# Moving key loads, two weight tiles' conversions and three operand loads in a fused attention and MLP kernel

## The chip, the cores and the metric

The kernel runs on one core of a Trainium2 chip, as one launch. The metric is device time in microseconds (us). A core has five engines that run their own instruction streams: TensorE (PE in the profile; its weight loads are PEld), VectorE (DVE), ScalarE (ACT), GpSimd (POOL) and SyncE (SP), which here only issues DMA transfers. The streams wait for each other through semaphores.

## The reference

Attention over four batches and eight heads (576 positions, 64 wide) with a decay from cumulated logarithms and a causal mask; its result, 2304 x 512, goes through two feed-forward layers. The weights of both layers arrive as float64, and the kernel converts them itself from their words.

```
scores = scale * q @ k.T                      # per head, 576 x 576
decay  = cum[:, None] - cum[None, :]          # cum = cumsum(log(clip(f, 1e-4, 1)))
attn   = softmax(where(causal, -1e9, scores + decay)) @ v
x      = attn, heads side by side             # 2304 x 512
h      = maximum(x @ w_in, 0)                 # 2304 x 2048
x      = (h * h) @ w_out                      # 2304 x 512
y      = (sigmoid(x @ w_gate) * (x @ w_val)) @ w_out2
```

## The kernel before

Each matmul operand is held as a high and a low part (fp32r), and a product takes three matmuls: high by high, high by low, low by high. Large products are made with seven block products in place of eight. The instruction order on each engine is the order in which the program calls the instructions (a manual schedule), and nearly every load and store goes through SyncE's one queue, in order. A DMA transfer also takes one of eight completion lanes in turn (DMAHW0 to 7).

**Attention** handles 16 pairs of heads p. A list, `ORDER`, gives the steps of one iteration with a lag in pairs, so three pairs are in work at a time. `load(p, which)` (L319) issues the loads of a pair: q and v in three pieces each (L335 twice, L339), k from the fourth pair on in four pieces for a transpose on DVE (L329). q and k have two buffers each, so pair p + 2 reuses the buffer of pair p. `cr_load` (L343) brings the decay rows of a pair into `cr`; in the setup these rows come from DVE's scan, in `pts`. `TQ` (L488) transposes q on TensorE and then loads q of pair p + 2; `TKv` transposes k on DVE; `kl` (L537) subtracts k's high part on POOL and then loads k of pair p + 2.

**The up stage** (first layer, x by w_in, relu and square) has eight blocks u of ten groups. A group is 12 matmuls (L240), then relu and square on ACT (L252, L253), block sums on DVE (L213), and stores of the `gt` tiles to DRAM by `g_spill` (L226; tiles of ten buffers). Beside it runs a list of weight pieces, `units`: a piece is loaded (L118 or L123) into one of two raw buffers, converted by ACT (L132) and four DVE operations (L150 to L160), and then, by its kind, made into high and low parts `hl` of w_in (ACT L179, POOL L183), kept as w_out, or stored to DRAM again as a gate or value tile (L862). A block has four pieces, two of w_in for the next block and two of w_out, or five, with a gate or value tile at the end.

**The down stage** (by w_out) has 84 steps of 12 matmuls (L1145): seven products k, three column ranges jj, four depth pieces w. Step i takes a tile `gl` loaded from DRAM (`d_load`, L819, three buffers) and split into high and low parts `gg` (`d_split`: ACT L825, then DVE L826, three buffers). Loop i splits for step i + 2. The first three loads and splits stand in the last block of the up stage. After step 3 the sums of the first product are copied by ACT and DVE out of PSUM into `pa0`, a tile in memory that the up stage used. The order of the loads in this loop:

```
        if i == NW - 1:
            g_spill(len(spill))
...
        while loaded[1] <= i + (4 if 57 <= i < 78 else 3):
...
            d_load(loaded[1])
            loaded[1] += 1
        if i == 2:
            g_spill(len(spill) // 2)
        if i > 0:
            d_split(i + 2)
```

The stages behind these, the gated layer and the output product, are not touched.

Of the kernel before, what the change touches and what calls it, by code (L numbers as in the profile page):

```python
# [41 lines left out]
def kernel(  # L42
# [17 lines left out]
    NP = BH // 2  # L60
# [250 lines left out]
    TP = 3  # L311
# [59 lines left out]
    def setup():  # L371
        nc.vector.memset(qk[1]["kh"].bitcast(F32)[:, 0:256], 0.0)
        nc.vector.memset(one_l.bitcast(F32), 0.0)
        for r in range(2):
            nc.vector.memset(one_l.bitcast(F32)[64 * r:64 * r + 64, 128 * r:128 * r + 128], 1.0)
        nc.vector.memset(cum_s.bitcast(F32)[:, 2 * S:3 * S], 0.0)
        for t in sm_t:
            nc.vector.memset(t[:, 9:13], 1.0e-9)
        nc.vector.memset(nm_t[0][:, 9:11], 0.0)
        for r in range(2):  # L380
            nc.vector.memset(nm_t[0][64 * r:64 * r + 64, 9 + r:10 + r], 1.0)
        busy(16)
        nc.sync.dma_start(out=f_sb, in_=f.rearrange("b h s -> (b h) s"))
        make_identity(nc, ident)
        for nm_ in "qk":
            for t in nat[nm_]:
                nc.gpsimd.memset(t[64:128, NF, :, :], 0.0)
        nc.scalar.activation(out=sm_t[0][0:1, 0:1], in_=one_l.bitcast(F32)[0:1, 0:1], func=AF.Ln)
        load(0, "qk", nc.scalar)
        nc.vector.tensor_scalar(f_sb, f_sb, 1.0e-4, 1.0, op0=ALU.max, op1=ALU.min)  # L390
        nc.vector.tensor_reduce(out=nm_t[0][:, 0:1], in_=ident[:, 0:111:22], axis=mybir.AxisListType.X, op=ALU.add)
        nc.vector.tensor_scalar(one_l, one_l.bitcast(F32), nm_t[0][:, 0:1], None, op0=ALU.mult)
        nc.scalar.activation(out=f_sb, in_=f_sb, func=AF.Ln)
        nc.scalar.activation(out=sm_t[0][0:BH, 0:1], in_=f_sb[:, 0:1], func=AF.Exp)
        nc.vector.tensor_tensor_scan(out=cum_f, data0=f_sb, data1=f_sb, initial=0.0, op0=ALU.add, op1=ALU.min)
        nc.vector.tensor_copy(cum_s[:, 0:S], cum_f)
        nc.vector.tensor_tensor(
            out=cum_s[:, S:2 * S], in0=cum_f, in1=cum_s.bitcast(F32)[:, 0:S], op=ALU.subtract
        )
        for d in qk:  # L400
            nc.gpsimd.memset(d["cr"].bitcast(F32), 0.0)
        for t in nat["v"]:
            nc.gpsimd.memset(t[64:128, NF, :, :], 0.0)
        for t in pt_t:
            nc.gpsimd.memset(t[:, 2 * POFF[NF] + S:2 * POFF[NF] + PC], 0.0)
        cum_v = cum_s.bitcast(F32).rearrange("p (t s) -> p t s", t=3)
        load(1, "q")
        cr_load(0, cum_v)
        load(1, "k")
        cr_load(1, cum_v)  # L410
        nc.gpsimd.memset(maskc, 0.0)
        nc.gpsimd.affine_select(
            out=maskc[:, MD:MD + 128], in_=maskc[:, MD:MD + 128], pattern=[[-1, 128]],
            compare_op=ALU.is_ge, fill=BIG, base=0, channel_multiplier=1,
        )
        for r in range(2):
            nc.gpsimd.affine_select(
                out=maskc[64 * r:64 * r + 64, S - REM:S], in_=maskc[64 * r:64 * r + 64, S - REM:S],
                pattern=[[-1, REM]], compare_op=ALU.is_ge, fill=BIG, base=0, channel_multiplier=1,
            )  # L420
# [67 lines left out]
    def TQ(p):  # L488
        x = ps2()
        if p < TP:  # L490
            live["kt", p] = ps2()
        if p > 2:
            live["s4", p - 1] = ps2()
            s4_decay(p - 1)
        live["q", p] = transpose_in(nat["q"][p % 2], x)
        if p + 2 < NP and p != 1:
            load(p + 2, "q")

    def qh(p):
# [37 lines left out]
    def kl(p, late):  # L537
        if late == (p < TP):
            d, eng = qk[p % 2], nc.vector if late else nc.gpsimd
            eng.tensor_tensor(out=d["kl"], in0=live.pop(("k", p)), in1=d["kh"].bitcast(F32), op=ALU.subtract)  # L540
            if not late and p + 2 < NP:
                load(p + 2, "k")

    def S01(p):
        s = live.pop(("s01", p))
# [197 lines left out]
    for it in range(min(lags), NP + max(lags)):  # L743
# [6 lines left out]
        for nm_, lag in steps:  # L750
            p = it - lag
# [79 lines left out]
    for u in range(NU):  # L831
        us = [("in", 2 * u + 2), ("in", 2 * u + 3)] if u < NU - 1 else []
        us += [("out", 2 * u), ("out", 2 * u + 1)]
        if 1 <= u <= 4:
            us.append((("gate", 0), ("gate", 1), ("val", 0), ("val", 1))[u - 1])
        at0 = (0, 3, 5, 7, 9) if len(us) == 5 else (0, 3, 6, 9)
        for x, o in zip(us, at0):
            for ph in range(3):
                when.setdefault(2 * GU * u + 2 * GU * (o + ph) // 12, []).append((len(units), ph))
            units.append(x)  # L840
    NX = len(units)
    loaded = [0, 6]
# [241 lines left out]
    for i, (k_, jj, w) in enumerate(steps):  # L1084
        if i == NW - 1:
            g_spill(len(spill))
            u1.close()
            gts.close()
            wi0.close()
            at_p = dn.enter_context(tc.tile_pool(name="at", bufs=2, side="right", reuse_waits="tile"))  # L1090
            wtmp_p[0] = w2s.enter_context(tc.tile_pool(name="tmp2", bufs=4, reuse_waits="tile"))
            raws = [raw_p.tile([128, 1024], F32, tag="raw", name=f"raw{n}") for n in range(2)]
            wt_p = w2s.enter_context(tc.tile_pool(name="wt", bufs=1, reuse_waits="tile"))
            wring = []
            pus = ExitStack()
            pu_p = pus.enter_context(tc.tile_pool(name="pu", bufs=1, reuse_waits="tile"))
            pu = {}
            for n in (1, 2, 3, 0):
                t = pu_p.tile([128, 4, BT], F32, tag=f"pa{n}", name=f"pa{n}")
                pu[n, 0], pu[n, 1] = t[:, 0:2, :], t[:, 2:4, :]  # L1100
            for n in range(3):
                pu[n, 2] = pu_p.tile([128, 2, BT], F32, tag=f"pb{n}", name=f"pb{n}")
            dd.update({n: t_src(3, n) for n in range(2)})
            dd[2], gl_more = (t[:, 0:2 * BT].rearrange("p (c t) -> p c t", c=2) for t in raws)
        if i == 57:
            gl_free.insert(0, gl_more)
        while loaded[1] <= i + (4 if 57 <= i < 78 else 3):
            if loaded[1] > 81:
                gl_free[:] = [t for t in gl_free if t is not gl_more]
# [3 lines that stand above are left out]
            g_spill(len(spill) // 2)  # L1113
        if i > 0:
            d_split(i + 2)
        if i == 8:
            wf_sums(NW - 1, nc.vector)
        if i in SUBS:
            n, wc = SUBS[i]
            a11, a2 = part(wc, 0, 0), part(wc, 1, n)  # L1120
            nc.vector.tensor_tensor(out=a11 if n else a2, in0=a2, in1=a11, op=ALU.subtract)
        if k_ < 6:
            if jj == 1 and w == NW - 1:
                prep_sums(k_ + 1, 0)
            if jj == 2:
                if w < NW - 1:
                    prep_sums(k_ + 1, w + 1)
                prep(k_ + 1, w)
        if late:
            late.pop(0)()  # L1130
        if i == K6:
            fa, fb = (
                wf_p.tile([128, 1024 * n], F32R, tag=f"wf{x}", name=f"f{x}") for x, n in enumerate((5, 3))
            )
            tt[0, 2], tt[0, 3], tt[0, 4] = quad(fa[:, 0:1536]), quad(fa[:, 1536:3072]), quad(fb[:, 0:1536])
            wring.append([t.rearrange("p (h n) -> p h n", h=2) for t in (fb[:, 1536:3072], fa[:, 3072:5120])])
        for fn in D1X.get(i, ()):
            fn()
        ws, s = aop[k_, w], gg.pop(i)
        for u in range(2):  # L1140
            for c in range(2):
                o = bank((BASE[k_] + 2 * jj + c) % 8)[:, 0:BT]
                cs = slice(c * 128, (c + 1) * 128)
                for x, (a, b_) in enumerate(((0, 0), (0, 1), (1, 0))):
                    nc.tensor.matmul(  # L1145
                        o, lhsT=ws[:, a, u, cs], rhs=s[:, b_, u, :],
                        start=(k_ in (0, 2, 5) and w == u == x == 0), stop=(w == NW - 1 and u == 1 and x == 2),
                        skip_group_check=k_ in (1, 3, 4, 6),
                    )
                if w == NW - 1 and u == 1:  # L1150
                    d_post(k_, jj, c, o)
# [183 lines left out]
    for n, (z, key, m) in enumerate(items):  # L1335
# [12 lines left out]
        elif m % 2:  # L1348
            at(*slot(z + 6), *[part_fn(w_sum, key, m // 2, x) for x in range(4)])
            for x in range(4):  # L1350
                p = 42 * (m // 2) + x - 1
# [353 lines left out]
```

## Time and profile before

| what | value |
|---|---|
| time, median of 3 runs | 946.87 us (946.37 to 947.45) |
| the profiled execution's own time | 948.93 us |
| its span, first to last instruction | 947.1 us |
| TensorE busy | 938.8 us, 99% of the span |
| VectorE busy | 731.7 us, 77% |
| ScalarE busy | 553.6 us, 58% |
| GpSimd busy | 308.8 us, 33% |
| TensorE clock granted | 1.00 of full speed over the run |

The profile is of one execution. Attention lasts until about 175 us, the up stage until 367, the down stage until 543, the gated layer and the output product to the end. Shares of busy time are averages over these stages; the time follows the engine that the others wait for in each, and that is TensorE almost everywhere.

### The profile page before, as it was taken

To read this page: it belongs to the slowest core of one execution; us is meant where nothing else is said; L and a number is where in the kernel's file an instruction comes from. 1 tells how busy PE (TensorE), PEld (TensorE's weight loads), DVE (VectorE), ACT (ScalarE), POOL (GpSimd) and SP (SyncE) were. 2 spreads that over 40 slices of the span, in tenths; PEclk is the share of its full clock that TensorE was granted. 3 is DMA by queue.
4 is the path that set the end of the run, shared out by engine and by line. 5 is a ranking of instruction groups with operands and counts; after the bars stand their busy time and mean duration, and the time that the engine had idled before them with its cause. 6 is when DMAs were issued, how large, how long until landed. Compare 5 with 4: busy or idle time off the path is not lost.

```text
span 947.1 us, 17435 instructions
## 1 busy us (share of the span) xinstructions
PE 938.8 (99%) x6058; PEld 872.4 (92%) x6058; DVE 731.7 (77%) x1485; ACT 553.6 (58%) x1113; POOL 308.8 (33%) x384
## 2 busy tenths in 40 slices
PE   8999999999999999999999999999999999999998
PEld 7888888888888889999999999999999999889998
DVE  8999998267666766787888988767666677698895
ACT  7889998366655665556566565544445455353432
POOL 7898998012121110010002446524344342200000
PEclk9999999999999999999999999999999999999999
DMA  5654440388888989767776512433333346864441
GB/s 126 145 120 93 91 80 14 101 263 261 281 261 282 288 287 315 209 196 210 227 236 194 149 64 95 139 115 126 121 113 126 136 151 212 258 217 140 150 133 69
DMA packets 185167, 160.83 MB, mean 170 GB/s; under 512 B 81112, under 2 KB 158252, under 8 KB 185080
## 3 DMA queue, kind: packets, MB, share of 16 engines
q1 hardware_dynamic: 184648, 159.54, 56.0%
q8 instruction: 47, 0.77, 0.3%
q14 instruction: 40, 0.33, 0.1%
q10 hardware_dynamic: 432, 0.20, 0.1%
HBM read 102.93 MB, written 56.73 MB: 169 GB/s over the span
## 4 chain that ended last, share of the span: by engine, by line
PE 77%; DMA 8%; DVE 6%; ACT 3%; issue 3%; POOL 2%; SPq 1%; DVEq 0%; ACTq 0%; POOLq 0%
PE ps L1199 27%; PE ps L1145 17%; PE ps L1545 9%; PE ps L240 5%; PE pa L646 4%; PE pa L475 4%; PE ps L1421 3%; PE pa L612 3%; DMA gl<-g 2%; DMA g<-gt 2%; DMA wraw<-in_moe_w_in_dram 2%; DVE gt L213 1%; DVE wtmp L155 1%; PE pa L240 1%; ACT gt L253 1%
## 5 line engine op out<-in xcount | busy, mean ns | idle before, releaser
L240 PE MATMUL ps<-xT,hl 128*128 128x512 f32 (+1 forms) x912 | 186.8, 367 | 0.3 <-POOL hl L183 0.3
L240 PEld LDWEIGHTS ps<-xT,hl 128*128 128x128 f32 x912 | 158.2, 189 | 28.9 <-POOL hl L183 0.7
L1145 PE MATMUL ps<-gg,ao 128*128 128x384 f32 x1008 | 175.6, 334 | 0.6 <-DVE gg L826 0.6
L1145 PEld LDWEIGHTS ps<-gg,ao 128*128 128x128 f32 x1008 | 174.6, 188 | 1.4 <-DVE gg L826 1.0
L601 POOL TENSOR_TENSOR pt<-pt,sm 128x128 f32<-128x128 f32 (+2 forms) x142 | 104.5, 767 | 16.8 <-DVE sm L593 15.0
L1199 PE MATMUL ps<-xT,r 128*128 128x384 f32 x576 | 107.6, 334 | 0.0
L825 ACT ACTIVATE gg<-gl 128x768 fp32r<-128x768 f32 x78 | 66.0, 846 | 61.4 <-PE ps L1145 36.1
L1199 PEld LDWEIGHTS ps<-xT,r 128*128 128x128 f32 x576 | 100.6, 188 | 0.1
L826 DVE TENSOR_TENSOR gg<-gl,gg 128x768 fp32r<-128x768 f32 x78 | 77.2, 992 | 28.0 <-ACT gg L825 27.6
L213 DVE TENSOR_TENSOR gt<-gt 128x512 f32<-128x512 f32 (+1 forms) x96 | 49.3, 558 | 55.1 <-ACT gt L253 54.7
L457 ACT ACTIVATE pt<-pt,nm 128x384 f32<-128x384 f32 (+2 forms) x144 | 82.8, 579 | 3.9 <-DVE nm L449 3.9
L449 DVE CUSTOM_DVE_ANT_0 pt<-pa,maskc 128x384 f32<-128x384 f32 (+2 forms) x144 | 67.1, 515 | 1.6 <-PE pa L475 1.3
L132 ACT ACTIVATE wtmp<-wraw 128x512 f32<-128x512 f32 x66 | 43.8, 664 | 38.4 <-DMA wraw<-in_moe_w_in_dram 13.9
L183 POOL TENSOR_TENSOR hl<-wf,hl 128x512 fp32r<-128x512 f32 x14 | 18.1, 1294 | 126.8 <-ACT hl L179 126.8
L1199 PE MATMUL ps<-xT,f 128*128 128x384 f32 x288 | 55.7, 334 | 0.0
L1199 PE MATMUL ps<-t,r 128*128 128x384 f32 x288 | 54.1, 334 | 0.0
L1199 PEld LDWEIGHTS ps<-xT,f 128*128 128x128 f32 x288 | 50.5, 188 | 0.0
L1199 PEld LDWEIGHTS ps<-t,r 128*128 128x128 f32 x288 | 50.3, 188 | 0.1
L253 ACT ACTIVATE gt<-gt 128x512 f32<-128x512 f32 (+1 forms) x80 | 47.2, 590 | 2.5
L155 DVE SCALAR_TENSOR_TENSOR wtmp<-wraw,wtmp 128x512 int32<-128x512 int32 (+1 forms) x68 | 46.4, 683 | 1.6
L1523 ACT ACTIVATE xT<-x 128x896 fp32r<-128x896 f32 x27 | 25.8, 954 | 36.8 <-DMA x<-g 15.2
L646 PE MATMUL pa<-pts,vn 128*64 128x320 f32 (+4 forms) x448 | 46.8, 360 | 0.0
(260 smaller groups left out, 1896.5 us busy)
## 6 DMA issues: line engine op xcount, KB each, us to landing
gl<-g SPq DMA_DIRECT2D x90, 384.0 KB
g<-gt SPq DMA_DIRECT2D x120, 256.0 KB
wraw<-in_moe_w_out_dram SPq DMA_DIRECT2D x28, 512.0 KB
x<-g SPq DMA_DIRECT2D x72, 128.0 KB
wraw<-in_moe_w_in_dram SPq DMA_DIRECT2D x16, 512.0 KB
wraw<-in_moe_w_val_dram SPq DMA_DIRECT2D x12, 512.0 KB
g<-pb SPq DMA_DIRECT2D x29, 192.0 KB
wraw<-in_moe_w_gate_dram SPq DMA_DIRECT2D x10, 512.0 KB
```

The source lines that it names most:

```text
L213: nc.vector.tensor_tensor(out=o, in0=a, in1=b_, op=ALU.subtract)
L240: nc.tensor.matmul(h, lhsT=a, rhs=x[b_], start=(c == 0 and i == 0), stop=(c == KD - 1 and i == 2))
L253: nc.scalar.activation(out=r, in_=r, func=AF.Square)
L449: nc.vector.tensor_tensor_reduce(out=o, in0=s, in1=mask, scale=1.0, scalar=3.0e38, op0=ALU.add, op1=ALU.min, accum_out=scol(p, nm_t, c),)
L457: nc.scalar.activation(out=x, in_=x, func=AF.Exp, bias=scol(p, nm_t, c), scale=-1.0, accum_out=scol(p, sm_t, c))
L601: nc.gpsimd.tensor_tensor(out=x, in0=x, in1=scol(p, sm_t, c).to_broadcast([128, e - a]), op=ALU.mult)
L646: nc.tensor.matmul(o[64 * h:64 * h + 64, 512 * half + s - lo:512 * half + hi - lo], lhsT=vn[:, c, h, :], rhs=pts[:, h * PW + c * PS + s:h ...
L825: nc.scalar.activation(out=s[:, 0], in_=t, func=AF.Copy)
L826: nc.vector.tensor_tensor(out=s[:, 1], in0=t, in1=s.bitcast(F32)[:, 0], op=ALU.subtract)
L1145: nc.tensor.matmul(o, lhsT=ws[:, a, u, cs], rhs=s[:, b_, u, :], start=(k_ in (0, 2, 5) and w == u == x == 0), stop=(w == NW - 1 and u == 1 ...
L1199: nc.tensor.matmul(o, lhsT=w[p][:, a, ws], rhs=operand(n, jj, b_, c), start=(first and c == x == 0), stop=(c == 1 and x == 2), skip_group_ ...
L1545: nc.tensor.matmul(o, lhsT=YR[i % 4][:, a, FROM[n]], rhs=b_op(n, u, b_), start=(x == u == y == 0), stop=(u == NU2 - 1 and y == 2), skip_gr ...
```

## The change

In the setup, all loads of q and k of the second pair are issued ahead of the decay rows of the first two pairs. In attention, for pairs p from 3 on (`TP` is 3), the load of q of pair p + 2 stands behind the load of k in `kl`, not in `TQ`. In the up stage the four gate and value tiles are pieces of blocks 1, 3, 5 and 6, not 1 to 4. In the down stage, in loops 1 to 3, the load for step i + 5 is issued directly behind the split for step i + 2, ahead of the remaining stores.

```diff
-        load(1, "q")
-        cr_load(0, cum_v)
-        load(1, "k")
-        cr_load(1, cum_v)
+        load(1, "qk")
+        for p in range(2):
+            cr_load(p, cum_v)
...
-        if p + 2 < NP and p != 1:
+        if p < TP and p != 1:
             load(p + 2, "q")
...
             if not late and p + 2 < NP:
                 load(p + 2, "k")
+                load(p + 2, "q")
...
-        if 1 <= u <= 4:
-            us.append((("gate", 0), ("gate", 1), ("val", 0), ("val", 1))[u - 1])
+        if u in (1, 3, 5, 6):
+            us.append({1: ("gate", 0), 3: ("gate", 1), 5: ("val", 0), 6: ("val", 1)}[u])
...
         if i > 0:
             d_split(i + 2)
+        if 0 < i < 4:
+            d_load(i + 5)
+            loaded[1] += 1
```

TensorE's order stays as it is. On SyncE in the setup, rows of the order before (-) and of the change (+); `qn` and `kn` are buffers of q and k, `cr_163` the decay rows of the first pair:

```order
 L335 DMA qn_153<-in_q_dram 128x4x64 x2
 L339 DMA qn_153<-in_q_dram 64x2x64
-L346 DMA cr_163<-pts 6x1x576
 L335 DMA kn_155<-in_k_dram 128x4x64 x2
 L339 DMA kn_155<-in_k_dram 64x2x64
+L346 DMA cr_163<-pts 6x1x576
 L346 DMA cr_168<-pts 6x1x576
```

The first pair's decay rows move behind three issues of k. On SyncE in attention, one iteration; `vn` is v, `wraw` a raw piece of w_in:

```order
 L118 DMA wraw<-in_moe_w_in_dram 128x4x256
 L346 DMA cr_163<-cum_d 6x576
 L335 DMA vn_157<-in_v_dram 128x4x64 x2
 L339 DMA vn_157<-in_v_dram 64x2x64
-L335 DMA qn_152<-in_q_dram 128x4x64 x2
-L339 DMA qn_152<-in_q_dram 64x2x64
 L329 DMA kn_154<-in_k_dram 32x18x32 x4
+L335 DMA qn_152<-in_q_dram 128x4x64 x2
+L339 DMA qn_152<-in_q_dram 64x2x64
 L118 DMA wraw<-in_moe_w_in_dram 128x4x256
```

The three issues of q move behind the four of k. On SyncE at the start of the down stage; `g1` is the DRAM copy of the up stage's tiles, and the loads into gl0, gl1 and gl2 are those for steps 6, 7 and 8:

```order
 L226 DMA g1_3_61<-gt_4463 128x512
 L226 DMA g1_3_61<-gt_4454 128x512
+L819 DMA gl0_2701<-g1_2_60 128x2x384
 L226 DMA g1_3_61<-gt_4478 128x128 x2
+L819 DMA gl1_2702<-g1_3_61 128x2x384
 L226 DMA g1_3_61<-gt_4483 128x4x128
 L226 DMA g1_3_61<-gt_4478 128x128
-L819 DMA gl0_2701<-g1_2_60 128x2x384
-L819 DMA gl1_2702<-g1_3_61 128x2x384
 L819 DMA gl2_2703<-g1_0_58 128x2x384
```

Loads 6 and 7 move ahead of the last stores, and the store of gt_4483 stands behind load 7, its place in the lanes being DMAHW5 now. On ACT at the same place, with the semaphores that a row waits for: before,

```order
L825 ACTIVATE gg_4576<-gl2_2703 128x768 [waits DMAHW4_49,DVE_49,PE_49]
L483 ACTIVATE pa0_4571<-ps0_2682 128x384 [waits DMAHW0_49,DMAHW2_49,DVE_49,PE_49]
L825 ACTIVATE gg_4594<-gl0_2701 128x768 [waits DMAHW5_49,DVE_49,PE_49]
L825 ACTIVATE gg_4610<-gl1_2702 128x768 [waits DMAHW6_49,DVE_49,PE_49]
```

and with the change,

```order
L825 ACTIVATE gg_4577<-gl2_2703 128x768 [waits DMAHW4_49,DVE_49,PE_49]
L482 ACTIVATE pa0_4573<-ps0_2682 128x384 [waits DMAHW5_49,DMAHW3_49,DMAHW6_49,DVE_49,PE_49]
L825 ACTIVATE gg_4595<-gl0_2701 128x768 [waits DMAHW1_49,DVE_49,PE_49]
L825 ACTIVATE gg_4610<-gl1_2702 128x768 [waits DMAHW4_49,DVE_49,PE_49]
```

The rows stand in the same order (splits 5, copy into pa0, splits 6 and 7); the copy's waits are for other lanes, and the splits' too.

## Rows read from the trace of the kernel before

**Rows 1.** The page, part 1: busy us, share of the span, instructions.

```profile
PE 938.8 (99%) x6058; PEld 872.4 (92%) x6058; DVE 731.7 (77%) x1485; ACT 553.6 (58%) x1113; POOL 308.8 (33%) x384
```

**Rows 2.** Waits of TensorE: us in total, times, longest.

```profile
...
PE pa L612 <- DVE xT L661: 0.5, 1, 0.5
...
PE ps L240 <- POOL hl L183: 0.3, 1, 0.3
...
```

**Rows 3.** Windows: us, each engine's busy time, granted clock, DMA share, GB/s.

```profile
230.00:280.00 50.00, 50.00 (x245) 42.36 (x244) 33.77 (x64) 27.58 (x52) 6.96 (x7) 1.00 0.86 274
280.00:330.00 50.00, 49.71 (x242) 41.82 (x241) 34.47 (x65) 32.16 (x59) 6.70 (x6) 1.00 0.87 276
...
375.00:385.00 10.00, 9.45 (x53) 8.94 (x52) 4.12 (x6) 3.91 (x6) 0.00 (x0) 1.00 0.80 252
385.00:450.00 65.00, 65.00 (x377) 65.00 (x376) 53.69 (x76) 39.33 (x58) 4.18 (x4) 1.00 0.71 203
```

**Rows 4.** Timeline of SyncE in the setup: start, us, instruction, count.

```profile
4.53 0.77 SPq L339 DMA_DIRECT2D qn<-in_q_dram  x1
6.90 0.81 SPq L346 DMA_DIRECT2D cr<-pts  x1
7.77 0.94 SPq L335 DMA_DIRECT2D kn<-in_k_dram  x2
```

**Rows 5.** Timeline at 9.4 us, weight loads; in brackets idle and releaser.

```profile
9.36 0.21 PEld L475 LDWEIGHTS pa<-cr,one_l 64*128 64x128 f32 x2 [0.17 <-issue]
```

**Rows 6.** The chain in attention: start, us, what.

```profile
45.95 2.37 DMA kn<-in_k_dram
```

**Rows 7.** Timeline of POOL in attention.

```profile
40.61 1.41 POOL L540 TENSOR_TENSOR kl<-kn,kh 128x576 fp32r<-128x576 f32 x1
```

**Rows 8.** Timeline of SyncE in attention.

```profile
44.30 2.15 SPq L329 DMA_DIRECT2D kn<-in_k_dram  x4
```

**Rows 9.** Timeline of DVE in attention.

```profile
48.45 0.78 DVE L530 STREAM_TRANSPOSE kn<-kn 128x576 f32<-128x576 f32 x1 [1.19 <-DMA kn<-in_k_dram]
```

**Rows 10.** Timeline of TensorE: one pair of matmuls in three iterations.

```profile
41.84 0.39 PE L475 MATMUL pa<-cr,one_l 64*128 64x512 bf16 x2
...
52.28 0.39 PE L475 MATMUL pa<-cr,one_l 64*128 64x512 bf16 x2
...
62.02 0.39 PE L475 MATMUL pa<-cr,one_l 64*128 64x512 bf16 x2
```

**Rows 11.** Timeline of POOL, up stage: low halves that open blocks 4, 5, 6.

```profile
290.38 1.30 POOL L183 TENSOR_TENSOR hl<-wf,hl 128x512 fp32r<-128x512 f32 x1 [9.18 <-ACT hl L179]
...
316.33 1.29 POOL L183 TENSOR_TENSOR hl<-wf,hl 128x512 fp32r<-128x512 f32 x1 [19.75 <-ACT hl L179]
...
338.20 1.29 POOL L183 TENSOR_TENSOR hl<-wf,hl 128x512 fp32r<-128x512 f32 x1 [4.86 <-ACT hl L179]
```

**Rows 12.** Timeline of ACT, end of the up stage.

```profile
359.15 0.60 ACT L252 ACTIVATE gt<-ps 128x512 f32<-128x512 f32 x1 [3.22 <-DMA g<-gt]
```

**Rows 13.** Timeline of SyncE, start of the down stage.

```profile
367.64 0.41 SPq L819 DMA_DIRECT2D gl<-g  x1
368.24 5.63 SPq L226 DMA_DIRECT2D g<-gt  x8
373.97 7.60 SPq L819 DMA_DIRECT2D gl<-g  x5
```

**Rows 14.** Timeline of DVE, start of the down stage: split 3.

```profile
370.34 0.95 DVE L826 TENSOR_TENSOR gg<-gl,gg 128x768 fp32r<-128x768 f32 x1
```

**Rows 15.** Timeline of ACT, start of the down stage: first copy, split 6.

```profile
374.65 0.49 ACT L483 ACTIVATE pa<-ps 128x384 f32<-128x384 f32 x1 [0.64 <-DMA g<-gt]
378.34 0.85 ACT L825 ACTIVATE gg<-gl 128x768 fp32r<-128x768 f32 x1 [3.19 <-DMA gl<-g]
```

**Rows 16.** The chain, start of the down stage: the load before.

```profile
367.64 5.42 DMA gl<-g
```

**Rows 17.** Timeline of TensorE, start of the down stage.

```profile
380.23 4.97 PE L1145 MATMUL ps<-gg,ao 128*128 128x384 f32 x27 [0.55 <-DVE gg L826]
```

## Prediction

> **What bounds the kernel now.** First the page's busy times [rows 1]: TensorE works 938.8 of 947.1 us. All that an edit of order can win is the remainder, so I read where TensorE waits. The waits by releaser [rows 2] name, in the places that the change touches, 0.5 us in attention on DVE's transposed sums (L661) and 0.3 us in the up stage on POOL's low halves (L183). The third touched place, the first steps of the down stage, I read from windows [rows 3]: in 375–385 TensorE ran 53 matmuls, while 385–450 shows 377 in 65 us (5.80 a us, 58.0 in ten). Five missing matmuls at 0.172 us are 0.86 us. The same count gives the true size of the up stage's stall: 242 matmuls in 280–330 against 245 in 230–280, so 3 at 0.204 us = 0.61 us, though the wait is recorded as 0.3. The clock column reads 1.00 (2.4 GHz) in all of these stretches, so no term below has a clock in it. From 385 on weight loads fill 65.00 of 65 us: what TensorE has won or lost by then is carried to the end unchanged.
>
> **The sum's base.** The rows come from one execution of 948.93 us (span 947.1), 2.06 above the median of 946.87. Every term is a difference in the place where it arises, so I subtract the sum from the median, and expect a profiled execution about 2 us above it again.
>
> **1. Start: k ahead of the decay rows.** SyncE's queue [rows 4] ends q's last issue at 5.30; the first decay row's issue starts at 6.90, with nothing in the queue between, so it waits for its data. k's three issues take 0.94 + 0.77 us (the last is of the same form as q's last). Put ahead, with gaps of 0.05, they fill 5.35 to 7.1, and the decay row is issued at 7.1 instead of 6.90: +0.2. Who waits for it? TensorE's weight load from cr at 9.36 was idle 0.17 before [rows 5]. No row times this transfer's landing; the nearest, a k load in attention, took 2.37 us from issue [rows 6], which puts the landing at 9.27, behind the previous weights' end at 9.36 − 0.17 = 9.19. So the delay is on the path. I take +0.2, with bounds 0 (the idle has another cause) and +0.4 (the next instructions slip as well). The earlier k1 brings nothing that a row shows. *On this place by itself: the Trainium skill, "DMA: Bandwidth & Descriptors", section "Anatomy of one DMA — SWDGE (gpsimd) path", fits 2.0 us plus bytes / 436e3 per transfer, on a path other than this queue's. For 6x576 floats (13.8 KB) this estimate lands at 8.93, ahead of 9.19; the delay would cost nothing and the sum be 0.2 lower. The trace's 2.37 us speaks against it.*
>
> **2. Attention: k ahead of q.** What frees the buffer of the next k but one is POOL's kl, which ends at 42.02 [rows 7]. Three issues of q stand ahead of k's four on SyncE, so these begin at 44.30 [rows 8]. Behind it, k can go 2.28 us earlier. DVE's transpose waits 1.19 us for k's landing [rows 9], so its wait goes with 1.09 to spare. TensorE's loss there is read from the period of a fixed matmul pair [rows 10]: 10.44 us across the stall against 9.74 in the next iteration, so −0.70. The recorded 0.5 [rows 2] is the low bound. The price is q, later by about k's 2.15; it is first used in the next iteration's transposes, and the seven issues and the others of an iteration fill well under its 9.74, so I cost it at nothing. Without that cover it would cost the same kind of stall, at most 0.7.
>
> **3. Up stage: the gate and value tiles in blocks 1, 3, 5, 6 instead of 1 to 4.** Every conversion on ACT, DVE and POOL from block 2 on shifts by a block with four or five pieces. POOL's low halves of the even pieces [rows 11] are 25.95 apart over a block of five and 21.87 over one of four: 4.08 per piece. The one that TensorE waits for (316.33) opens block 5. Ahead of it lay blocks 1 to 4 with five pieces each, now 5, 4, 5, 4: two pieces fewer, so it can start 8.2 earlier, at 308.1 or 308.2. The stall goes: −0.61, low bound the recorded 0.3 [rows 2]. The next one (338.20) opens block 6; block 5 has five pieces now for four, so one piece of the lead is given back and it starts at 334.1, 4.1 earlier. The price is block 6: its fifth piece, 4.08 long, now stands directly ahead of the down stage. The lead of 4.1 just pays for it, so I take 0; without it the whole 4.1 arrives at the transition.
>
> **4. Transition: three loads directly behind splits.** The down stage stops at step 6, which starts at 380.23 after the chain of its late load. The loads stand on SyncE behind eight g stores, at 373.97 [rows 13]; ACT's split of that load starts at 378.34 after 3.19 idle [rows 15]. Now load 6 stands directly behind split 3, whose subtraction ends at 371.29 [rows 14], so 2.7 earlier: by itself more than the stall of 0.86. But load 7 is also moved ahead of the store of gt_4483 (the order's third piece), and the order of ACT shows who waits for that store: the first copy into pa0, which reuses the gt tiles' memory, has now a wait for DMAHW5, the lane of that store, and stands ahead of split 6 on ACT. Step by step: load 6 at 371.3; its issue 0.4; two stores at 5.63/8 = 0.70 each; load 7 at 373.1, 0.4; the store at 373.5 to 373.8. Landing: 4.3 us (373.97 to 378.3 [rows 13, 15]) to 5.42 [rows 16], so 377.8 to 379.2. Then copy 0.49, split 0.85, subtraction 0.97, gaps 0.1: step 6 at 380.2 to 381.6, middle 380.9, against 380.23 [rows 17], with the end of the up stage as before. How much earlier this end comes is unknown: nothing, if the fifth piece eats the lead, up to 3.2, ACT's idle for a g store there [rows 12]. I take the middle, 1.6, since TensorE itself arrives 1.1 earlier by terms 1 to 3: step 6 at 379.3, **net −0.9**. A floor for TensorE: 380.23 − 0.86 − 0.61 − 0.70 + 0.2 = 378.3, net −2.0.
>
> So 946.87 − 0.9 = **946.0**; a profiled execution at 948.0. A measurement of this kernel can tell about 0.2%, 1.9 us, from no change, so even the floor is just at that limit.
>
> **The rivals.** *All three stalls gone, and only +0.2 paid*: the store lands early enough (below 375.9, within 2.4 us of issue as k's load did [rows 6]) or the up stage ends over 2.6 earlier: 944.8, faster (by 2.0 to 2.2 if the start costs nothing). Against it: transfers of that stretch took 4.3 to 5.4. *The change doesn't do what it says at the transition*: the new wait for the store takes the place of the old wait for the load, all of the lead and more: step 6 at 379.9 to 382.1, middle 380.9, so 947.5, between −0.3 and +1.9, the same by measurement. For it: landing of 5.4 and no lead at ACT. *Slower*: the fifth piece of block 6 is paid in full at the transition. Low half 338.20 must come 4.1 earlier to cover it; step 6 passes 382.1 (+1.9) when that lead falls short by the 1.2 which separate 380.9 from 382.1, below 2.9, that is where the low half starts later than 335.3. Paid whole, from 380.9: +0.7 + 4.1, 951.7; about 949 to 951.7. Against it: ACT still idles 3.22 us at once at the end of the stage [rows 12].
>
> **How the numbers follow.** The forecast (−0.3 to −1.85) gets 0.46: two of three stalls are simple and off each other's way. All gone, 0.24. New wait takes all, 0.22; slower, 0.08. So faster by over 0.2% is 0.24, within it 0.46 + 0.22 = 0.68, slower 0.08. The range reaches from the floor with no cost at the start (946.87 − 2.2 = 944.6) to 1.1 above the time before (948.0), which leaves out the upper half of the new wait's case and the slower one.
>
> **What would show it.** Right: the weight load from cr at about 9.5; no wait of DVE for k ahead of its transpose, and a period of 9.75 where 10.44 stood; no TensorE wait for POOL's hl, with low halves at about 308 and 334; at the transition, ACT's first copy into pa0 idle, released by a g store, and a short TensorE wait for gg behind it. Wrong: no idle of ACT there and 58 matmuls in every ten us (all gone); low half later than 335.3, or step 6 past 382.1 (slower). The prediction falls most easily at the transition, by when the store of gt_4483 lands, or if another instruction of block 6 sets the start of the down stage.

## The result

The changed kernel is slower: 953.67 us (median of 6 runs, 952.14 to 954.32) against 947.25 us for the kernel before on the same chip (946.37 to 949.02). The ratio is 1.0063, with a 95% interval of 1.0050 to 1.0076. The forecast was 946.0, so about 0.9 us to be won; about 6.0 us were lost. The profiled execution has a span of 952.2 us, 5.1 above the span before.

I read the new profile in the order of the prediction. First the waits of TensorE (total us, times, longest):

```profile
PE ps L1148 <- ACT gg L825: 3.0, 1, 3.0
...
PE ps L1148 <- DVE gg L826: 1.1, 2, 0.5
PE ps L1148 <- ACT gt L252: 0.8, 1, 0.8
```

The waits of [rows 2], on DVE's xT and on POOL's hl, are gone. In their place three waits stand at L1148, the down stage's matmul (its line is 1145 before). So the first three terms came as forecast in kind, and the loss lies in the down stage's first steps: at step 12 TensorE is 5.66 us later than before (398.32 for 392.66). About 0.6 of that comes back further on, and it belongs to no edit: from step 12 to the end the profiles of this case take 553.9 to 554.5 us, with 554.5 before and 553.9 here. Windows (us, busy time of each engine, granted clock, DMA share, GB/s):

```profile
375.00:380.00 5.00, 5.00 (x31) 4.94 (x29) 0.96 (x1) 0.85 (x1) 0.00 (x0) 1.00 1.05 367
380.00:385.00 5.00, 1.43 (x7) 0.91 (x6) 2.29 (x3) 2.69 (x4) 0.00 (x0) 1.00 0.35 114
385.00:390.00 5.00, 5.00 (x21) 5.00 (x20) 1.92 (x3) 1.19 (x2) 0.00 (x0) 0.66 0.75 236
390.00:395.00 5.00, 5.00 (x30) 5.00 (x30) 4.44 (x7) 3.53 (x6) 0.00 (x0) 1.00 0.56 159
```

From 380 to 385 TensorE runs 7 matmuls where some 30 fit. Behind that it is busy all of the time, and yet runs 21: the granted clock has fallen to a mean of 0.66. That is nine or ten matmuls at about 0.165 us, some 1.6 us, which no wait shows. TensorE's own rows at the start of the down stage:

```profile
365.73 0.69 PE L1148 MATMUL ps<-gg,ao 128*128 128x384 f32 x3
367.20 6.17 PE L1148 MATMUL ps<-gg,ao 128*128 128x384 f32 x34 [0.78 <-ACT gt L252]
373.90 6.36 PE L1148 MATMUL ps<-gg,ao 128*128 128x384 f32 x35 [0.53 <-DVE gg L826]
383.28 0.44 PE L1148 MATMUL ps<-gg,ao 128*128 128x384 f32 x1 [3.02 <-ACT gg L825]
384.28 18.02 PE L1148 MATMUL ps<-gg,ao 128*128 128x384 f32 x93 [0.55 <-DVE gg L826]
```

TensorE reaches the stage at 365.73, 0.92 earlier than before (366.65). It then loses 0.78 and 0.53 in the first steps, and at step 6 waits 3.02 and 0.55. The chain says for what (start, us, what):

```profile
376.33 0.44 SPq L819
...
376.81 1.15 SPq L226
...
378.01 4.02 DMA g<-gt
382.02 0.05 ACT pa L482
...
382.40 0.84 ACT gg L825
...
383.26 0.97 DVE gg L826
```

A store (g from gt) lands at 382.0; only then ACT makes the first copy into pa0 (L482), and behind it split 6. (The chain hangs the landing on the second of two stores, issued at 378.01. The program's waits, read below, name the first, issued at 376.81.) Queues of SyncE and ACT at this place, and DVE's splits 3 and 4:

```profile
351.22 0.38 SPq L123 DMA_DIRECT2D wraw<-in_moe_w_out_dram  x1
...
373.98 0.88 SPq L819 DMA_DIRECT2D gl<-g  x1
...
376.81 1.70 SPq L226 DMA_DIRECT2D g<-gt  x2
```

```profile
358.12 0.66 ACT L132 ACTIVATE wtmp<-wraw 128x512 f32<-128x512 f32 x1 [5.22 <-DMA wraw<-in_moe_w_out_dram]
...
382.01 0.49 ACT L482 ACTIVATE pa<-ps 128x384 f32<-128x384 f32 x1 [5.84 <-DMA g<-gt]
```

```profile
372.89 1.82 DVE L826 TENSOR_TENSOR gg<-gl,gg 128x768 fp32r<-128x768 f32 x2
```

Two things are to be seen. Load 6 leaves at 373.98, no earlier than in [rows 13], though it now stands directly behind split 3: split 3 itself ends at 373.8, not at 371.29 as in [rows 14]. And the end of the up stage is late on ACT: the conversion of a w_out piece starts at 358.12. Before, the same piece was asked for at 348.67 and converted at 354.12:

```profile
348.67 0.33 SPq L123 DMA_DIRECT2D wraw<-in_moe_w_out_dram  x1
```

```profile
354.12 0.66 ACT L132 ACTIVATE wtmp<-wraw 128x512 f32<-128x512 f32 x1 [2.48 <-DMA wraw<-in_moe_w_out_dram]
```

So there are two suspects: a late end of the up stage, and a copy that waits for a store. The experiments part them. Theory A (late tail): the fifth piece in block 6 is all of it. Theory B: the loads' edit put stores behind loads, and the copy waits for them. Theory C: it takes both. Theory M came after the first four runs.

### The profile page after: what moved, and what is told of

Read it like the earlier page. It is cut to its first block, busy times and chain, and to the rows that moved or that the text cites. A ratio compares the mean times of both kernels' runs of the same rounds, so it can differ in the third digit from the quotient of the medians.

```text
span 952.2 us, 17421 instructions
## 1 busy us (share of the span) xinstructions
PE 940.9 (99%) x6058; PEld 875.0 (92%) x6058; DVE 732.0 (77%) x1485; ACT 554.2 (58%) x1113; POOL 309.4 (32%) x384
## 4 chain that ended last, share of the span: by engine, by line
PE 89%; DMA 4%; DVE 3%; ACT 1%; issue 1%; POOL 1%; SPq 0%; DVEq 0%; ACTq 0%; POOLq 0%
PE ps L1202 28%; PE ps L1148 17%; PE ps L240 13%; PE ps L1548 9%; PE ps L1424 5%; PE pa L646 5%; PE pa L474 4%; PE pa L612 3%; DMA g<-gt 2%; DMA wraw<-in_moe_w_out_dram 1%; PE pa L240 1%; PE pa L581 1%; PE pa L430 1%; PE pa L618 1%; DVE gt L213 1%
## 5 line engine op out<-in xcount | busy, mean ns | idle before, releaser
L1148 PE MATMUL ps<-gg,ao 128*128 128x384 f32 x1008 | 177.9, 337 | 4.9 <-ACT gg L825 3.0
L1148 PEld LDWEIGHTS ps<-gg,ao 128*128 128x128 f32 x1008 | 176.2, 189 | 6.4 <-ACT gg L825 3.3
```

The lines of the kernel that those rows point to most:

```text
L1148: nc.tensor.matmul(o, lhsT=ws[:, a, u, cs], rhs=s[:, b_, u, :], start=(k_ in (0, 2, 5) and w == u == x == 0), stop=(w == NW - 1 and u == 1 ...
```

## Experiments

All ratios are to the kernel before on the same chip, with 95% intervals. Step 6 shows twice in TensorE's rows, with its first matmul, which waits for ACT's half of the split, and with the next, which waits for DVE's; before they stood at 379.23 and 380.23.

### The four parts alone

**a_start** has only the setup's edit:

```diff
-        load(1, "q")
-        cr_load(0, cum_v)
-        load(1, "k")
-        cr_load(1, cum_v)
+        load(1, "qk")
+        for p in range(2):
+            cr_load(p, cum_v)
```

> The start alone: k of the second pair ahead of the decay rows. In the changed kernel a fixed pair of matmuls in attention stands 0.35 us later than before (42.19 for 41.84). If that is the decay rows' later landing, this kernel alone shows the same shift and +0.35 us (ratio 1.0004, not told from 1 by timing, but by the trace). If it is the scatter of one execution, the pair stands at 41.84 +- 0.1. Neither theory on the transition expects anything there.

Ratio 0.9995 (0.9986 to 1.0004). The fixed pair stands at 42.16, +0.32. The weight loads show that it is the decay rows that are late, and not something ahead of them:

```profile
8.48 0.19 PEld L474 LDWEIGHTS pa<-kl,qh 64*128 64x128 f32 x2
...
9.68 0.21 PEld L474 LDWEIGHTS pa<-cr,one_l 64*128 64x128 f32 x2 [1.00 <-issue]
```

kl's weights come at 8.48, and those from cr still wait until 9.68 ([rows 5] has 9.36). The fixed pair by itself would not show it: u_again, with the old start, has it at 42.10 once, though its weights from cr come at 9.37. In this execution attention had no stall either: the period at 42 us was 9.75.

**a_q** has only `q` behind `k` in `TQ` and `kl`.

> q behind k alone: the period of the fixed pair across the stall goes from 10.44 to 9.74 us, and the time falls by 0.7 (ratio 0.9993). A rival would have the stall come back at a later q: then a period over 9.8 further on, and no gain.

Ratio 1.0003 (0.9992 to 1.0014): no change that can be measured. The trace shows the period of 9.74 at the place, and no later one above 9.75. But the stall itself is not a constant. Five profiled kernels have attention as before, and their periods there are 10.44, 9.78, 10.61, 10.39 and 10.21: a stall between 0.04 and 0.87, mean 0.55. The edit takes away something that was a part of most of these executions only.

**a_units** has only the blocks of the gate and value pieces:

```diff
-        if 1 <= u <= 4:
-            us.append((("gate", 0), ("gate", 1), ("val", 0), ("val", 1))[u - 1])
+        if u in (1, 3, 5, 6):
+            us.append({1: ("gate", 0), 3: ("gate", 1), 5: ("val", 0), 6: ("val", 1)}[u])
```

> The gate and value pieces in blocks 1, 3, 5, 6 alone, loads as before. Theory A (late tail: the fifth piece of block 6 makes ACT, DVE and the transfers late at the end of the up stage, and all of the loss is that): the subtractions of the first three splits end about 2.5 us later than before, step 6 starts at 383 to 385, +3 to +5 us with the clock's fall. Theory B (new wait: the loss is that stores stand behind the loads moved forward): no loss here, -0.6 to 0. Theory C (it takes both): a late tail, but a stall under 2.5 us, no fall of the clock, 0 to +2 us.

Ratio 1.0032 (1.0021 to 1.0043), +3.0 us. Step 6 of TensorE, and the window behind it:

```profile
380.22 0.45 PE L1145 MATMUL ps<-gg,ao 128*128 128x384 f32 x1 [1.94 <-ACT gg L825]
381.21 20.95 PE L1145 MATMUL ps<-gg,ao 128*128 128x384 f32 x111 [0.55 <-DVE gg L826]
```

```profile
380.00:385.00 5.00, 4.23 (x14) 3.97 (x15) 2.88 (x3) 1.99 (x4) 0.00 (x0) 0.66 0.60 180
```

Half of the loss, and none of the theories has it right. The splits' subtractions are later by under 1 us, not 2.5. Step 6 begins 0.99 later than before, behind a longer wait, since TensorE arrived 1.3 earlier; and the clock falls. ACT's rows hold a surprise:

```profile
378.21 0.49 ACT L483 ACTIVATE pa<-ps 128x384 f32<-128x384 f32 x1 [3.89 <-DMA g<-gt]
379.33 0.84 ACT L825 ACTIVATE gg<-gl 128x768 fp32r<-128x768 f32 x1 [0.62 <-DMA gl<-g]
```

The copy into pa0 waits for a late store here too, without the loads' edit.

**a_loads** has only the three loads:

```diff
+        if 0 < i < 4:
+            d_load(i + 5)
+            loaded[1] += 1
```

> The three down loads behind splits alone, pieces in blocks 1 to 4. Theory A: no loss, step 6 at 379.5 to 381, -0.9 to +0.7. Theory B: the copy into pa0 waits for the last store, step 6 at 383 or later, TensorE's stall 3 us and the clock down behind it, +3 to +6 us. Theory C: the copy waits, but under 2.5 us more than before, 0 to +2 us.

Ratio 1.0001 (0.9992 to 1.0009). Step 6 has no stall at all:

```profile
368.07 34.14 PE L1148 MATMUL ps<-gg,ao 128*128 128x384 f32 x196
```

```profile
376.07 0.49 ACT L483 ACTIVATE pa<-ps 128x384 f32<-128x384 f32 x1 [0.71 <-PE ps L1148]
```

Theory B falls: with the same order of stores and loads on SyncE the copy waits for TensorE alone. TensorE reached the stage 1.4 us later here (368.07), which by itself leaves less to wait for; b_no_units, at the end of the experiments, comes as early as the whole change and has no stall either. The two parts that cost 3.0 and 0 alone cost 6.0 together.

### The memory under pa0

The programs' waits tell why. The ACT row of the first copy, with its lanes, in the kernel with the loads alone and with the pieces alone:

```
L483 ACTIVATE pa0_4573<-ps0_2682 128x384 [waits DMAHW0_49,DMAHW2_49,DVE_49,PE_49]
L483 ACTIVATE pa0_4571<-ps0_2682 128x384 [waits DMAHW3_49,DMAHW6_49,DVE_49,PE_49]
```

Traced back through the counts, the first waits for the stores of gt_4382 and gt_4431, done early; the second for the store of gt_4483 (DMAHW3), the last but one, and for one done early (DMAHW6). In the whole change DMAHW5 is the store of gt_4483, and the two other lanes are early stores. The tiles' addresses agree: pa0 takes the bytes 129152 to 135295 of a partition in both; gt_4483 lies at 118912 with the old blocks and at 131200 with the new. So the moved pieces changed which buffer the pool gave to that tile. Theory M: the loss that only the two parts together show is the copy's wait for a store which the pieces put under pa0 and the loads put behind load 7.

**c_swap** is the whole change with pa0 in other memory; **c_units_swap** is a_units with the same line.

```diff
-            for n in (1, 2, 3, 0):
+            for n in (0, 2, 3, 1):
```

> The whole change, but pa0 lies in other memory: the tiles pa1 and pa0 are allocated in exchanged places, so that the first copy into pa0 no longer lands on the buffer from which gt_4483, the store behind load 7, is read. Theory M (memory: the pieces' new blocks put gt_4483 under pa0, and the copy waits for that store, which the loads' edit moved back): the copy runs within 0.8 us of split 5, step 6 starts at 379.5 to 381, no fall of the clock, 4 to 6 us won back against the whole change, ratio 0.999 to 1.002. Theory A (late tail from the fifth piece of block 6): step 6 still at 382.5 to 384, ratio 1.005 or more.

Ratio 1.0002 (0.9991 to 1.0013): the loss of 0.63% is down to nothing that can be measured, by a line that changes no instruction's place in any order.

```profile
376.44 0.47 ACT L482 ACTIVATE pa<-ps 128x384 f32<-128x384 f32 x1
380.19 0.84 ACT L825 ACTIVATE gg<-gl 128x768 fp32r<-128x768 f32 x1 [3.28 <-PE ps L1148]
```

```profile
381.09 0.44 PE L1148 MATMUL ps<-gg,ao 128*128 128x384 f32 x1 [0.89 <-ACT gg L825]
```

The copy runs at 376.44, directly behind split 5, and the clock stays at 1.00. Split 6 now stands until 380.19. Its row names TensorE, but step 3, whose buffer it takes (three buffers), had ended by 375.9, so what it waits for is load 6, issued at 373.97. In the whole change the split began at 382.40: beyond the load, the copy's wait cost 2.2. Against the whole change TensorE is 2.20 earlier at step 6 and 3.80 at step 12 (394.52 for 398.32), so the clock cost 1.6. Step 6 is still later than forecast (381.09 for at most 381), behind a stall of 0.89 and earlier ones of 0.74 and 0.53: the late tail remains.

> The pieces in blocks 1, 3, 5, 6 alone, and pa0 exchanged with pa1. In the run with these pieces alone the copy stood until 378.21 for a store, but split 6 stood until 379.33 for its load, issued at 374.55 behind all stores. Theory M says that there the load is last, so nothing is won: step 6 at 380.2, the clock falls, ratio 1.002 to 1.004. If the copy's wait was the last one after all: step 6 at 379.3 or earlier, ratio under 1.001.

Ratio 1.0033 (1.0023 to 1.0044), as theory M expects: without the loads' edit it is load 6 that comes last, so the copy's memory is worth nothing there. Two details missed: step 6 began at 381.45, not 380.2, and the clock did not fall in this profile, with a wait of 1.76 where a_units had 1.94. The profiled execution took 950.60, where the median of twelve is 952.40, so it does not tell whether the clock fell in the others; the ratio is that of a_units.

**d_loads_over** is the reverse: a_loads, with pa0 put onto the buffers of gt_4478 and gt_4483, by `for n in (1, 0, 3, 2)`.

> The loads' edit alone with the old blocks, but pa0 exchanged with pa1's neighbour so that it lies on the last stores' buffers (gt_4478, gt_4483). Theory M: the copy waits for the last store to land, 379.5 to 380.5, step 6 starts at 381.9 to 383 where the loads alone showed 380.55 without a stall: a stall of 1.3 to 2.5 us, and if the clock falls behind it 2 us more, ratio 1.001 to 1.005. Theory A: the same as the loads alone, ratio 1.000.

Ratio 1.0024 (1.0014 to 1.0033) where a_loads had 1.0001. The copy waits again, and step 6 with it:

```profile
379.32 0.49 ACT L483 ACTIVATE pa<-ps 128x384 f32<-128x384 f32 x1 [4.71 <-DMA g<-gt]
```

```profile
380.59 0.44 PE L1148 MATMUL ps<-gg,ao 128*128 128x384 f32 x1 [0.62 <-ACT gg L825]
```

The copy's wait is as forecast in kind. The stall is smaller than forecast, 0.62 and 0.55, and step 6 begins at 380.59, not 381.9 to 383: the stores had landed by 379.3, ahead of the forecast's 379.5 to 380.5. Here too the profiled execution, 949.71, lies below the median of 951.77. So the mechanism is there with the old blocks too, once the memory is made so.

### The fifth piece of block 6

**u_1345** keeps q behind k and the loads, leaves the start as before, and has the pieces in blocks 1, 3, 4, 5.

> A version for use: q behind k, the three loads, the old start, and the pieces in blocks 1, 3, 4, 5, so that block 6 keeps four. pa0 lies on gt_4382 and gt_4407, both stored ahead of the moved loads. Both theories expect no stall at step 6 and no fall of the clock; 0.5 to 2 us won, ratio 0.998 to 0.9995. If a stall stays in spite of both, a third cause is there.

Ratio 0.9972 (0.9962 to 0.9983). It beats both kernels, by 2.7 us against the kernel before, where 0.5 to 2 were forecast. No wait of TensorE is left at the down stage's start:

```profile
365.39 36.94 PE L1149 MATMUL ps<-gg,ao 128*128 128x384 f32 x212
```

**u_again** is the same kernel measured again, beside e_ops2 below.

> The version with pieces in blocks 1, 3, 4, 5, once more, beside the one above on the same chip: ratio 0.9965 to 0.998 as before; no stall at step 6.

Ratio 0.9979 (0.9970 to 0.9988).

**u_1345_noloads** is u_1345 without the loads' edit.

> The same version without the three loads' edit: q behind k and pieces in blocks 1, 3, 4, 5. If the loads behind splits are worth what the stall of before was (0.86 us, or more since TensorE now comes to the down stage 1.2 us earlier): step 6 at 379.5 to 380.3 for 377.87, a stall of 1.5 to 2.5, ratio 0.9985 to 1.000. If load 6 was not what held it: no stall, ratio 0.997.

Ratio 0.9999 (0.9990 to 1.0008), so the loads are worth 0.20 to 0.27% here, by the two measurements with them. Load 6 stands behind eight stores again, TensorE stalls 0.97 and 0.55 (forecast 1.5 to 2.5), and the clock falls behind it to a mean of 0.66 in 380 to 385, 20 matmuls for 30:

```profile
373.20 2.12 SPq L820 DMA_DIRECT2D gl<-g  x3
```

```profile
378.99 0.44 PE L1146 MATMUL ps<-gg,ao 128*128 128x384 f32 x1 [0.97 <-ACT gg L826]
```

```profile
380.00:385.00 5.00, 5.00 (x20) 5.00 (x21) 2.35 (x3) 1.69 (x2) 0.00 (x0) 0.66 0.73 223
```

**e_traffic** adds to u_1345, in block 6, a fifth piece that moves data and computes next to nothing (POOL fills a tile with zeros, DVE copies one column); **e_ops** one that makes the five conversion operations over words in memory and moves nothing. In the cut, the first two rows stand in both and the last in e_ops alone; its rows that call the conversion are left out.

```diff
+        if u == 6:
+            us.append(("pad", 0))
...
+            if key == "pad":                                  # e_traffic alone
+                if ph == 0:
+                    cv[n] = wtmp_p[0].tile([128, 512], F32, tag="tmp", name="wtmp")
+                    nc.gpsimd.memset(cv[n], 0.0)
+                elif ph == 1:
+                    nc.vector.tensor_copy(cv[n][:, 0:1], wraw.pop((key, m))[:, 0:1])
+                else:
+                    load_units(min(n + 3, NX))
+                    nc.sync.dma_start(out=w_d[key, m], in_=cv.pop(n))
...
+                wraw["pad", 0] = wsub(0, 0).rearrange("p a n -> p (a n)")   # e_ops, no load
```

> The version with pieces in blocks 1, 3, 4, 5, and in block 6 a fifth piece that only moves data: the 512 KB load into a raw buffer, one element read by DVE, and the 256 KB store of a tile of zeros into memory that nothing reads. pa0 stays on early stores. Theory T1 (the val piece in block 6 is paid through its transfers and its turn of the raw buffers: the next w_out piece is issued later and lands later): the conversion of that piece starts 3 to 4 us later, step 6 moves from 377.87 to 380 to 382, 2 to 4 us slower than the version without it, ratio to before 0.9995 to 1.002. Theory T2 (it is the five operations on ACT and DVE): under 1 us slower, ratio 0.997 to 0.998.

Ratio 1.0040 (1.0028 to 1.0053), 5.8 to 6.4 us above the two measurements of u_1345, the base here: more than the forecast 2 to 4. The w_out piece is issued at 353.41 (the base has 348.61) and converted 5.9 later than in the base, and step 6 begins at 382.11 for 377.88. e_traffic, then the base:

```profile
358.98 0.66 ACT L133 ACTIVATE wtmp<-wraw 128x512 f32<-128x512 f32 x1 [7.58 <-DMA wraw<-in_moe_w_out_dram]
```

```profile
353.05 0.67 ACT L132 ACTIVATE wtmp<-wraw 128x512 f32<-128x512 f32 x1 [2.67 <-DMA wraw<-in_moe_w_out_dram]
```

> The same version with a fifth piece in block 6 that only computes: the conversion's operations on ACT and DVE over words that are in memory already, into a tile that nothing reads; no load, no store, no raw buffer. Theory T1: within 0.5 us of the version without it, step 6 at 377.9 to 378.5, ratio 0.997 to 0.998. Theory T2: step 6 at 380 or later, ratio 0.9995 to 1.002.

Ratio 1.0005 (0.9996 to 1.0014), also 2.5 to 3.1 us above the base, which theory T1 did not expect. But ACT idled 4.41 us for a load there, so it was not short of time: the extra entry had taken a turn in the list by which loads are asked for, and the w_out load left at 350.69. **e_ops2** gives that turn back (`n + 4` for `n + 3` ahead of the extra piece):

> As the piece that only computes, but the loads' turn is kept: the w_out piece behind it is asked for as if the extra piece were not in the list (in the earlier run it was issued at 350.69 for 348.61, a turn later, though the extra piece loads nothing). Theory T1 (turn and transfers): the conversion of that w_out piece starts within 1 us of 353.05, step 6 at 377.9 to 378.7, ratio 0.997 to 0.9985. Theory T2 (the operations themselves): it starts at 355.5 or later, step 6 stalls as in the earlier run, ratio 1.0000 to 1.001.

Ratio 0.9981 (0.9972 to 0.9989), beside 0.9979 for u_again on the same chip. The five operations cost nothing that can be measured, and the w_out piece is converted on time:

```profile
352.69 0.68 ACT L133 ACTIVATE wtmp<-wraw 128x512 f32<-128x512 f32 x1 [0.57 <-DMA wraw<-in_moe_w_out_dram]
```

T2 falls. The late tail is made of a load's turn, which e_ops shows without any added transfer, and, for the rest of e_traffic's loss, of a later turn together with the transfers, which these runs do not part.

**b_no_units** is the whole change with the old blocks.

> The whole change with the pieces back in blocks 1 to 4: start, q behind k, three loads. Theory M and the late tail both say that the whole loss is gone: step 6 without a stall, low halves' stall as before, ratio 0.9985 to 1.0005. If a loss over 0.1% stays, a part of it is in the other edits.

Ratio 0.9994 (0.9984 to 1.0004): the loss is gone, and no gain can be told. In this profile the low halves' stall, expected as before, is missing too, so TensorE comes to the down stage as early as in the whole change. Load 6 leaves at 370.81, 3.2 us earlier than in [rows 13], and step 6 has no stall:

```profile
370.81 0.86 SPq L819 DMA_DIRECT2D gl<-g  x1
```

```profile
365.67 36.57 PE L1148 MATMUL ps<-gg,ao 128*128 128x384 f32 x210
```

## Why the prediction was wrong

**Term 1, start, +0.2.** Right in kind, a little small: +0.35 in the whole change, +0.32 alone, since the decay row left at 7.26 (a_start) and not at 7.1. The delay is on TensorE's path, as the row's 2.37 us said: from that issue to the weights at 9.68 it is 2.42. The fit that I weighed (the Trainium skill, "DMA: Bandwidth & Descriptors", section "Anatomy of one DMA — SWDGE (gpsimd) path") gives 2.03 by estimate, for another path, and would have had no delay; the runs of this queue disagree with it.

**Term 2, attention, −0.70.** The period came out as said, 9.74, but the size was read from one execution. Over five it is 0.55, and the time of the part alone shows nothing.

**Term 3, pieces, −0.61.** The low half that held TensorE starts at 309.47, later than the 308.1 forecast, and the stall is gone. It too was mis-sized by taking one profile: from the first up-stage matmul to the first down-stage matmul TensorE takes 201.9 us without the stall, and with the old blocks 202.48 (the profile of before), 204.14, 203.80, 203.76, 203.39 and once 201.91. The mean stall is 1.35, more than twice the term.

**Term 3's price, 0.** This step failed. "The lead of 4.1 just pays for it" counted the leads of low halves. These stand at 309.47 and, for the next one, at

```profile
335.29 1.29 POOL L183 TENSOR_TENSOR hl<-wf,hl 128x512 fp32r<-128x512 f32 x1 [8.65 <-ACT hl L179]
```

so the lead was 2.9, just where I put the turn to slower; but it was the wrong thing to count. The piece's price falls on what stands behind it in the raw buffers: the next w_out piece's load leaves at 351.22 for 348.67, 2.55 later, and its conversion starts 4.00 later, so from issue to use it took 1.45 longer. Why longer is not shown: the DMA share in 355 to 360 is 1.06 at 397 GB/s, but it was 1.07 at 378 GB/s before. ACT, DVE and the first splits stand behind that conversion in order. I had counted the piece as 4.08 us of operations, and not its transfers (512 KB in, 256 KB out) nor the raw buffer that it takes from the next load. Without this piece in block 6, u_1345 runs through step 6 at 377.88 and 378.05 without a stall; the floor of 378.3 without the start's 0.2 is 378.1.

**Term 4, transition.** This step failed twice. First, load 6 "2.7 earlier", and an end of the up stage 1.6 earlier on top: it stands behind split 3, and split 3 ended 2.5 later than before, as late as the tail, so the load left at 373.98, where it had left before. Where the tail is on time the reading holds (370.81 in b_no_units). Second, the copy's new wait. The prediction saw it in the order (DMAHW5, the store of gt_4483) and laid it to the loads' edit, with that store issued at 373.5 to 373.8. The experiments showed that the pieces' edit makes the wait, through the buffers; and the store was issued at 376.81, 3.0 or more later than that, where the sum had taken off another 1.6. Its landing took 5.2, within the 4.3 to 5.42 of the sum, so the sum's error is in when the store left. The prediction's sum for step 6 was 379.3. With the store's real landing it is copy at 382.0, split from 382.40 to 383.24, subtraction to 384.23, and TensorE at 384.28, as the rows show.

**What the prediction left out.** The clock. Behind the stall it fell, for 1.6 us here. The sentence that no term has a clock in it was right for the kernel before and wrong for the one forecast.

**The sum as measured.** From the whole change, other memory for pa0 gives back 0.61% of the time (3.80 us, 0.40%, in the traces, clock included; the difference of the two ratios has a spread of some 0.17%, so the two agree only roughly). Taking the last piece out of block 6, and the start back, gives a further 0.30%. The rival "slower", with the fifth piece paid at the transition, named the right place and got 0.08; it gave 949 to 951.7, and the copy's wait and the clock came on top. What remains open: why c_units_swap kept its clock at the same median as a_units, and how much of the 6 us of e_traffic is the turn of the raw buffers and how much the transfer; a kernel with a third raw buffer would tell, and was not tried.

## What to carry to other kernels

Moving work in the program's order can change which buffer a pool hands out, and so make an instruction far away wait for one of the last stores instead of an early one; read which stores a reused tile waits for, in each variant, before pricing the wait, and price the edits together as well as alone. The piece added ahead of a stage change was paid here by the transfers and buffer turns behind it, not by the operations that it added to engines that idle; count those first. A stall read from one profile is one draw: two of the three gains here were 0.7 and 0.6 in that profile, and 0.04 to 0.87 and 0 to 2.24 over several.

## What the runs showed of the hardware

The granted clock of TensorE fell behind the stall at step 6 in some profiles, to 0.50 (1.2 GHz) over a stretch of two us in three of them (the whole change, a_units and e_traffic) and to 0.56 in the fourth: behind waits of 3.02 (the whole change), 1.94 (a_units), 0.99 (e_traffic) and 0.97 us (u_1345_noloads), each with 0.55 more one matmul later. It stayed at 1.00 behind 1.76 (c_units_swap), 0.89 (c_swap) and 0.62 (d_loads_over). So the wait's length alone does not decide it. Two stretches, of the whole change and of c_units_swap:

```profile
386.00:388.00 2.00, 2.00 (x8) 2.00 (x8) 0.00 (x0) 0.36 (x1) 0.00 (x0) 0.50 1.06 373
382.00:384.00 2.00, 1.56 (x9) 1.56 (x10) 1.94 (x3) 1.27 (x2) 0.00 (x0) 1.00 0.23 24
```

The price in the whole change, by the matmuls that did not run and by its distance to c_swap, is 1.6 us.
